# Feed-forward layers with the features on partitions, and transposes done by DMA, in a four-layer forward and backward pass

## The chip, the cores and the metric

The kernel runs on one core of one Trainium2 chip. The metric is device time in microseconds (us): the median of three runs of the whole program. A separate execution was taken by the hardware profiler; it has a time of its own, and its trace is what the lines below come from.

Engine names as the profile prints them: PE is the matmul engine (PEld is its weight load, which overlaps PE), DVE the vector engine, ACT the scalar engine, POOL the GpSimd engine, SP the queue that issues every DMA of this kernel.

## What is computed

Two kinds of layer alternate, A, B, A, B, on an activation of 2048 tokens by 512, with a residual and a layer norm in front of each; the program returns the output and the gradients with respect to the input and all five weights.

```python
def _A_ref(x, wqkv, wo):        # linear attention, 32 heads of 16
    qkv = x @ wqkv              # phi(t) = where(t > 0, t + 1, exp(t)) + 1e-6
    kv, z = sum_s phi(k) v, sum_s phi(k)
    return ((phi(q) @ kv) / (phi(q) . z + 1e-6)) @ wo
def _B_ref(x, w_gate, w_up, w_down):   # feed-forward, F = 1376
    return (sigmoid(x @ w_gate) * (x @ w_up)) @ w_down
x = x + A(ln(x)); x = x + B(ln(x)); x = x + A(ln(x)); x = x + B(ln(x))
out, vjp = jax.vjp(f, A_x, A_wqkv, A_wo, B_w_gate, B_w_up, B_w_down); grads = vjp(grad_out)
```

The change concerns the B layers (layers 1 and 3 of 0 to 3).

## The kernel before, in words

Tokens are cut into 16 tiles of 128 (`NST`), the model width into 4 chunks of 128 (`NDC`), F = 1376 into 10 chunks of 128 and one of 96 (`NFC`), or into slices of 512, 512 and 352 columns (`FSL`). The order of the instructions of PE, ACT, DVE and POOL is the order in which the program emits them (`tc.manual_schedule`, lines 134 and 1042 on); each engine works through its list in that order. Only SP's order is set by a scheduler. DMAs take turns on eight semaphores, and each waits for the one eight places ahead of it.

**Forward, layers A then B.** `kq_fwd` makes q and k of all tiles and sums over tokens; `ab_fwd` (from line 844) then walks over 16 token tiles and, tile by tile, does the rest of layer A and all of layer B, in a pipeline: while tile st is in B, tiles st+1 to st+3 are in A. For one tile of B, `gu` (line 857) makes gate and up with tokens on partitions: the normalised activations hT are stationary, 512 or 352 columns of w_gate and w_up move; ACT makes sigmoid(g) (`ssd`) and sigmoid(-g) (`oms`), DVE multiplies u by the sigmoid (`hh`, line 869), POOL makes the second factor of the derivative (line 870). `transposes` (line 872) turns `hh` on PE in 11 blocks, ACT copies them out (`hhT`), and `finish` (line 885) multiplies by w_down one tile later. Woven in are the fronts of layer A's output: `front1` (line 776) and `front2` (lines 786 to 788: three DVE instructions that make the normalised q, `pqn`), `front3` (PE transposes `pqn`, ACT copies it), `attn_y` (4 matmuls, DVE adds the residual, then layer norm statistics on DVE and POOL). In the middle of the walk, one tile's order is gu slice 2, `front2`, the transposes of slice 1, `finish` of the tile before (11 matmuls), `front3`. `Fill` places PE transposes of the weights (`wT_groups_a`, `wT_groups_b`) in between; the transposed weights are stored in DRAM and loaded again later.

**Backward, layer B.** `b_bwd_p1` (from line 1038) walks over token tiles: the output gradient's transpose `gT` (4 PE transposes, line 1000), `dhh_mm` (gT stationary, w_down transposed moving, line 1008), two DVE products per slice (`dd`, line 1016), 22 PE transposes of `dd` (line 1083) copied out by ACT (line 1085), 22 matmuls of 512 columns (line 1117) one tile later, and the layer norm's backward. `hh` and `dd` go to DRAM in groups of 256 features (`hdd`, the last 96 in `hdl`).

**Weight gradients.** `p2_gen` takes jobs of 256 (or 96) features. A job loads a set (`p_set`, line 1242: 16 token tiles by 256 features, 1 MB) and multiplies it with all tokens of h or of the gradient: 32 matmuls of 512 columns for w_down (line 1330), 64 of 256 columns for w_up or w_gate (line 1342). There are three set buffers; in the walk over jobs the next sets are issued about two jobs ahead. Jobs of layer 3 fill PE in the backward of layer A (`A2.first`) and then run alone; those of layer 1 do the same at the end of the program.

Of the kernel before, what the change touches and what calls it, by code (L numbers as in the profile page):

```python
# [17 lines left out]
S = 2048  # L18
# [9 lines left out]
FSL = [(0, 512), (512, 512), (1024, F - 1024)]  # L28
# [7 lines left out]
def fchunks_of_slice(fs):  # L36
    c0, w = FSL[fs]
    return list(range(c0 // P, (c0 + w + P - 1) // P))


def fc_rows(fc):
    return FLAST if fc == NFC - 1 else P
# [18 lines left out]
def kernel(  # L61
# [42 lines left out]
    for l in range(4):  # L104
        d = {}
        d["h"] = dram.tile([S, D], BF16, name=f"sv_h{l}")
        d["gbf"] = dram.tile([S, D], BF16, name=f"sv_gbf{l}")
        if l % 2 == 0:
            for nm in ("hT", "pqn", "phq", "pk"):
                d[nm] = dram.tile([S, D], BF16, name=f"sv_{nm}{l}")  # L110
            d["dqk"] = dram.tile([2 * D // GW, P, NST, GW], BF16, name=f"sv_dqk{l}")
            d["X"] = dram.tile([D, D], BF16, name=f"sv_X{l}")
            for nm, w in SMALL:
                d[nm] = dram.tile([D, w], BF16, name=f"sv_{nm}{l}")
            d["MT"] = dram.tile([D, D], BF16, name=f"sv_MT{l}")
        else:
            d["ssd"] = dram.tile([S, 2, F], BF16, name=f"sv_ssd{l}")
            d["hdd"] = dram.tile([3, NG, P, NST, GW], BF16, name=f"sv_hdd{l}")
            d["hdl"] = dram.tile([3, P, NST, F - NG * GW], BF16, name=f"sv_hdl{l}")
        k.sv[l] = d  # L120
    k.wT = dict(
        wqkvT=dram.tile([3 * D, D], BF16, name="wqkvT_d"),
        woT=dram.tile([D, D], BF16, name="woT_d"),
        wgT=dram.tile([NFC * P, D], BF16, name="wgT_d"),
        wuT=dram.tile([NFC * P, D], BF16, name="wuT_d"),
        wdT=dram.tile([D, F], BF16, name="wdT_d"),
    )
# [5 lines left out]
    )  # L133
    k.rstd = [keep.tile([P, NST], F32, name=f"rstd_all{l}") for l in range(4)]
# [5 lines left out]
    with tc.tile_pool(name="wfwd", bufs=1, reuse_waits="tile") as wfwd, ExitStack() as lctx, tc.manual_schedule(engines=EM):  # L140
# [25 lines left out]
        def load_wd():  # L166
            nc.sync.dma_start(out=k.wd[:, 0:NFC - 1, :],
                              in_=B_w_down[0:(NFC - 1) * P, :].rearrange("(c p) j -> p c j", p=P))
            for r0, r1 in ((0, 64), (64, FLAST)):
                nc.sync.dma_start(out=k.wd[r0:r1, NFC - 1, :],  # L170
                                  in_=B_w_down[(NFC - 1) * P + r0:(NFC - 1) * P + r1, :])
# [9 lines left out]
            hT=lctx.enter_context(tc.tile_pool(name="ln_hT", bufs=4, reuse_waits="tile")),  # L181
# [3 lines left out]
        with tc.tile_pool(name="aq0", bufs=1, reuse_waits="tile") as aq:  # L185
            A = kq_fwd(k, aq, 0, lns[0], lns[1], x_bf)
            with tc.tile_pool(name="wt_stage", bufs=2, reuse_waits="tile") as wt_stage:
                fill = Fill(wT_groups_a(k, wt_stage))
                A.tail(fill)
                ab_fwd(k, A, lns[1], fill, nxt=lns[2])  # L190
        xctx.close()
        with tc.tile_pool(name="aq2", bufs=1, reuse_waits="tile") as aq:
            A = kq_fwd(k, aq, 2, lns[2], lns[3])
            hctx.close()
            wb = bctx.enter_context(tc.tile_pool(name="wbwd", bufs=1, side="right", reuse_waits="tile"))
# [4 lines left out]

            def out_cb(st):
                if st == NB:
                    k.pre["g"] = pre.tile([P, 2, D], BF16, name="pre_g")
                    nc.sync.dma_start(out=k.pre["g"][:], in_=dram_batch(g_in, 0, 2))
                    k.pre["ssd"] = pre.tile([P, 2, F], BF16, name="pre_ssd")
                    nc.sync.dma_start(out=k.pre["ssd"][:], in_=k.sv[3]["ssd"][rows(0), :, :])
                if st % 2 == 0:
                    ocur["t"] = k.ostg.tile([P, 2, D], BF16, name="out0_t", bufs=2)
# [7 lines left out]
            def last_cb(i):  # L216
                if i == 0:
                    k.pre["gT"] = pre.tile([P, NDC, P], BF16, name="pre_gT")
                    g_transposes(k, k.pre["g"][:, 0, :], k.pre["gT"])
                else:  # L220
                    k.pre["dd"] = pre.tile([P, 2, F], BF16, name="pre_dd")
                    for fs in range(2):
                        dd_ops(k, k.pre["dd"], k.pre["ssd"], fs, dhh_mm(k, k.pre["gT"], fs))
            fill = Fill(wT_groups_b(k, wb))
            A.tail(fill)
            ab_fwd(k, A, lns[3], fill, out_cb=out_cb, last_cb=last_cb)
# [5 lines left out]
    if True:  # L232
        def load_b_weights():
            k.wdT = wb.tile([P, NDC, F], BF16, name="wdT", tag="w_c")
            nc.sync.dma_start(out=k.wdT[:], in_=k.wT["wdT"].rearrange("(c p) f -> p c f", p=P))
            k.wuT = wb.tile([P, NFC, D], BF16, name="wuT", tag="w_a")
            k.wgT = wb.tile([P, NFC, D], BF16, name="wgT", tag="w_b")
            for t_sb, t_d in ((k.wuT, k.wT["wuT"]), (k.wgT, k.wT["wgT"])):
                nc.sync.dma_start(out=t_sb[:], in_=t_d.rearrange("(c p) j -> p c j", p=P))

# [5 lines left out]
        def load_a_weights(l):  # L246
            nc.sync.dma_start(out=k.X_ld, in_=k.sv[l]["X"].rearrange("(c p) j -> p c j", p=P))
            k.wqkvT = wb.tile([P, 3 * NDC, D], BF16, name="wqkvT", tag="w_a")
            nc.sync.dma_start(out=k.wqkvT[:], in_=k.wT["wqkvT"].rearrange("(c p) j -> p c j", p=P))
            woT_GT = wb.tile([P, 2, NDC, D], BF16, name="woT_GT", tag="w_b")  # L250
            k.woT, k.GT = woT_GT[:, 0, :, :], woT_GT[:, 1, :, :]
            nc.sync.dma_start(out=k.woT, in_=k.wT["woT"].rearrange("(c p) j -> p c j", p=P))
        k.load_b_weights, k.load_a_weights, k.load_MT = load_b_weights, load_a_weights, load_MT
# [6 lines left out]
        def mk_out1_cb(o1stg):  # L260
            o1cur = {}

            def out1_cb(st):
                if st % 2 == 0:
                    o1cur["t"] = o1stg.tile([P, 2, D], BF16, name="out1_t")
                nc.gpsimd.tensor_scalar(o1cur["t"][:, st % 2, :], k.xs[st][:], 1.0, 0.0, ALU.mult, ALU.add)
                if st % 2 == 1:
                    nc.sync.dma_start(out=dram_batch(out1, st // 2, 2), in_=o1cur["t"][:])
            return out1_cb
# [3 lines left out]
        A2, A0 = ABwd(k, R, 2), ABwd(k, R, 0, mk_out1_cb)  # L273
# [82 lines left out]
def wT_groups_a(k, stage):  # L356
    nc = k.nc
    groups = []
    for w_sb, wT_d, C in ((k.wqkv, k.wT["wqkvT"], 3 * D), (k.wo, k.wT["woT"], D)):
        for cc0 in range(0, C // P, 4):  # L360
            holder = {}
            for j in range(4):
                def g(bank, w_sb=w_sb, wT_d=wT_d, cc0=cc0, j=j, holder=holder):
                    if j == 0:
                        holder["t"] = stage.tile([P, 4, D], BF16, name="wt_st")
                    cc = cc0 + j
                    ps = ps_tile(k, bank, [P, 8, P], BF16, "wT_ps")
                    for rc in range(NDC):
                        nc.tensor.transpose(ps[:, rc, :], w_sb[:, rc, cc * P:(cc + 1) * P], k.ident[:])

                    def ev(eng):
                        evac_copy(k, holder["t"][:, j, :], ps[:, 0:NDC, :].rearrange("p a b -> p (a b)"), eng)
                        if j == 3:
                            nc.sync.dma_start(
                                out=wT_d[cc0 * P:(cc0 + 4) * P, :].rearrange("(n p) d -> p n d", p=P),
                                in_=holder["t"][:])
                    return ev
                groups.append(g)
    return groups


def wT_groups_b(k, wb):
    nc = k.nc
    groups = []
    k.wdT = wb.tile([P, NDC, F], BF16, name="wdT", tag="w_c")
    k.wuT = wb.tile([P, NFC, D], BF16, name="wuT", tag="w_a")
    k.wgT = wb.tile([P, NFC, D], BF16, name="wgT", tag="w_b")
    for cc in range(NDC):
        for fs in range(3):
            def g(bank, cc=cc, fs=fs):  # L390
                fcs = fchunks_of_slice(fs)
                ps = ps_tile(k, bank, [P, 8, P], BF16, "wT_ps")
                for i, fc in enumerate(fcs):
                    r = fc_rows(fc)
                    nc.tensor.transpose(ps[:, i, 0:r], k.wd[0:r, fc, cc * P:(cc + 1) * P], k.ident[0:r, 0:r])
                c0, w = FSL[fs]

                def ev(eng):
                    evac_copy(k, k.wdT[:, cc, c0:c0 + w], ps[:].rearrange("p a b -> p (a b)")[:, 0:w], eng)
                    if cc == NDC - 1 and fs == 2:  # L400
                        nc.sync.dma_start(out=k.wT["wdT"].rearrange("(c p) f -> p c f", p=P), in_=k.wdT[:])
                return ev
            groups.append(g)
    for w_sb, wT_sb, wT_d in ((k.wu, k.wuT, k.wT["wuT"]), (k.wg, k.wgT, k.wT["wgT"])):
        for cc in range(NFC):
            def g(bank, w_sb=w_sb, wT_sb=wT_sb, wT_d=wT_d, cc=cc):
                r = fc_rows(cc)
                if cc == 0:
                    nc.gpsimd.memset(wT_sb[FLAST:P, NFC - 1, :], 0.0)
# [31 lines left out]
class FwdLN:  # L441
# [34 lines left out]
    def pop(self, st):  # L476
        return self.hTs.pop(st)
# [1233 lines left out]
```

## Time and profile before

| | us |
|---|---|
| median of 3 runs | 1213.65 (1212.94 to 1217.52) |
| profiled execution, its own time | 1216.08 |
| its span, first to last instruction | 1214.3 |
| PE / PEld busy in the span | 1185.4 / 716.8 |
| DVE / ACT / POOL busy | 726.9 / 599.9 / 259.1 |
| DMA engines busy, share | 66% |
| forward of layer 1 (first gate matmul to last w_down matmul) | 76.1 to 223.7 |
| forward of layer 3 | 281.1 to 432.5 |
| backward of layer 3 (dhh to dh matmuls) | 428.3 to 569.5 |
| jobs of layer 3 alone | about 715 to 793 |
| backward of layer 1 | 793.1 to 930.6 |
| jobs of layer 1 and layer 0 alone | about 1072 to 1210 |

How to read it: a matmul's end is modelled, so PE's busy time says that PE had something in flight; what a matmul costs in a stream is the distance from one start to the next. In a timeline line, the first column is the start, the second the length of the merged piece, `x4` the number of instructions, and brackets at the end give idle time of the engine before the piece and who ended it.

### The profile page before, as it was taken

What the parts mean: (1) busy time and instruction counts of PE and PEld (TensorE: products, weight loads), DVE (VectorE), ACT (ScalarE), POOL (GpSimd) and SP (SyncE); (2) the same over time, 40 slices, a digit from 0 to 9 for tenths busy, and PEclk for the clock granted to TensorE, in tenths of its full rate; (3) what the DMA queues carried; (4) which work ended last, traced back from release to release, by engine and by line L of the source; (5) the groups of instructions that cost most, each with busy time, mean ns of one, the idle gap of its engine ahead of it and who ended that gap; (6) DMA issues with size and microseconds to landing.
All of it is one profiled execution on the core that took longest, in us unless ns stands there. A gap on an engine that the chain in (4) does not pass through costs nothing. (4 is left out here: it accounts for less than half of the span.)

```text
span 1214.3 us, 22436 instructions
## 1 busy us (share of the span) xinstructions
PE 1185.4 (98%) x8646; PEld 716.8 (59%) x8646; DVE 726.9 (60%) x1410; ACT 599.9 (49%) x1105; POOL 259.1 (21%) x467
## 2 busy tenths in 40 slices
PE   7989999998999999999999999999999999999998
PEld 4445555454555555555665566765556755577777
DVE  6778887777777556565786730056666966742221
ACT  5677776647767644445537631145445527620001
POOL 4236675204665410000110010000100101100000
PEclk9999999999999999999999999999999999999999
DMA  7934545435546696967866469687667766569974
GB/s 231 311 118 144 197 157 181 172 122 176 185 150 231 232 279 184 312 187 236 229 188 203 147 222 322 206 281 218 213 194 246 206 219 180 170 172 351 293 234 135
DMA packets 266203, 256.08 MB, mean 211 GB/s; under 512 B 43248, under 2 KB 250992, under 8 KB 261232
## 3 DMA queue, kind: packets, MB, share of 16 engines
q1 hardware_dynamic: 266096, 254.65, 66.0%
q8 instruction: 67, 1.10, 0.4%
q14 instruction: 40, 0.33, 0.1%
HBM read 135.69 MB, written 118.92 MB: 210 GB/s over the span
## 5 line engine op out<-in xcount | busy, mean ns | idle before, releaser
L1342 PE MATMUL p_ps<-p_set,p_a 128*128 128x256 bf16 (+1 forms) x1792 | 186.8, 263 | 0.0
L1016 DVE TENSOR_TENSOR dd<-dhh_ps,ssd 128x512 bf16<-128x512 f32 x144 | 82.5, 629 | 149.0 <-PE dhh_ps L1008 142.1
L1342 PEld LDWEIGHTS <-p_a 128*128 128x128 bf16 x1792 | 160.3, 98 | 18.7
L1085 ACT COPY ddT<-T_ps 128x1024 bf16<-128x1024 bf16 (+1 forms) x96 | 82.9, 868 | 126.5 <-PE T_ps L1083 126.5
L870 POOL TENSOR_TENSOR ssd_t<-hh_t,oms 128x512 bf16<-128x512 bf16 (+1 forms) x96 | 101.6, 1064 | 53.6 <-ACT out_t L212 40.9
L1117 PEld LDWEIGHTS <-ddT 128*128 128x128 bf16 (+1 forms) x704 | 66.4, 98 | 68.6
L864 PEld LDWEIGHTS <-hT 128*128 128x128 bf16 x768 | 71.2, 98 | 57.8 <-DVE hT L341 1.5
L982 POOL TENSOR_SCALAR ab<-c 128x2 f32<-128x2 f32 x64 | 12.5, 196 | 433.2 <-DVE junk L979 416.4
L864 PE MATMUL g_ps<-wg,hT 128*128 128x512 bf16 (+1 forms) x384 | 90.0, 357 | 1.1 <-DVE hT L341 1.1
L1321 DVE TENSOR_TENSOR dw_stg<-p_ps,dw_stg 128x512 bf16<-128x512 f32 (+2 forms) x43 | 28.4, 659 | 103.3 <-PE p_ps L1342 80.8
L864 PE MATMUL u_ps<-wu,hT 128*128 128x512 bf16 (+1 forms) x384 | 90.0, 357 | 0.0
L869 DVE TENSOR_TENSOR hh_t<-u_ps,ssd_t 128x512 bf16<-128x512 f32 (+1 forms) x96 | 61.0, 636 | 46.9 <-PE u_ps L864 26.7
L1117 PE MATMUL dh_ps<-wgT,ddT 128*128 128x512 bf16 (+1 forms) x352 | 86.2, 379 | 0.0
L1008 PE MATMUL dhh_ps<-wdT,gT 128*128 128x512 bf16 x372 | 82.5, 357 | 0.5 <-DVE dd L1016 0.5
L890 PE MATMUL y_ps<-wd,hhT 128*128 128x512 bf16 (+1 forms) x352 | 81.3, 379 | 0.6 <-DVE x L892 0.6
L1117 PE MATMUL dh_ps<-wuT,ddT 128*128 128x512 bf16 (+1 forms) x352 | 81.3, 379 | 0.0
L1330 PE MATMUL p_ps<-p_a,p_set 128*128 128x512 bf16 (+1 forms) x352 | 80.4, 379 | 0.0
L866 ACT ACTIVATE ssd_t<-g_ps 128x512 bf16<-128x512 f32 (+1 forms) x96 | 53.2, 554 | 31.7 <-PE g_ps L864 31.4
L974 ACT ACTIVATE t_sb<-dh_ps,rstd_all 128x512 f32<-128x512 f32 x64 | 44.0, 688 | 36.6 <-issue 18.4
L979 DVE SCALAR_TENSOR_TENSOR junk<-t_sb,h_ld 128x512 bf16<-128x512 f32 x60 | 41.2, 687 | 34.8 <-ACT t_sb L974 34.8
L1323 ACT CAST dw_stg<-p_ps 128x512 bf16<-128x512 f32 (+2 forms) x43 | 24.2, 563 | 72.1 <-PE p_ps L1342 51.8
L1330 PEld LDWEIGHTS <-p_set 128*128 128x128 bf16 (+1 forms) x352 | 34.4, 100 | 35.5
(236 smaller groups left out, 2184.9 us busy)
## 6 DMA issues: line engine op xcount, KB each, us to landing
p_set<-sv_hdd SPq DMA_DIRECT2D x30, 1024.0 KB, 6.4
sv_ssd<-ssd_t SPq DMA_DIRECT2D x32, 688.0 KB, 3.5
ssd<-sv_ssd SPq DMA_DIRECT2D x24, 688.0 KB, 5.0
sv_hdd<-dd SPq DMA_DIRECT2D x48, 320.0 KB, 3.3
sv_hdd<-hh_t SPq DMA_DIRECT2D x32, 320.0 KB, 2.6
p_set<-sv_dqk SPq DMA_DIRECT2D x8, 1024.0 KB, 5.4
h_ld<-sv_h SPq DMA_DIRECT2D x30, 256.0 KB, 4.5
p_a<-sv_h SPq DMA_DIRECT2D x12, 512.0 KB, 6.5
```

The costliest lines, as they stand in the source:

```text
L864: nc.tensor.matmul(ps[:, 0:w], lhsT=hT[:, kc, :], rhs=w_sb[:, kc, c0:c0 + w], start=(kc == 0), stop=(kc == NDC - 1))
L866: nc.scalar.activation(ssd_t[:, 0, c0:c0 + w], g_ps[:, 0:w], ACT.Sigmoid)
L869: nc.vector.tensor_tensor(hh_t[:, c0:c0 + w], u_ps[:, 0:w], ssd_t[:, 0, c0:c0 + w], ALU.mult)
L870: nc.gpsimd.tensor_tensor(ssd_t[:, 1, c0:c0 + w], hh_t[:, c0:c0 + w], oms[:, 0:w], ALU.mult)
L890: nc.tensor.matmul(y_ps[:], lhsT=T["hhT"][0:r, fc, :], rhs=k.wd[0:r, fc, :], start=(fc == 0), stop=(fc == NFC - 1))
L974: k.nc.scalar.activation(self.t[:], dh_ps, ACT.Identity, scale=rstd_col, accum_out=self.c12[:, 0:1])
L1008: k.nc.tensor.matmul(ps[:, 0:w], lhsT=gT[:, jc, :], rhs=k.wdT[:, jc, c0:c0 + w], start=(jc == 0), stop=(jc == NDC - 1))
L1016: k.nc.vector.tensor_tensor(dd[:, a, c0:c0 + w], ps[:, 0:w], ssd[:, a, c0:c0 + w], ALU.mult)
L1085: nc.scalar.copy(ddT[:, :, fcs[0]:fcs[0] + nfull, :], tps[:, :, 0:nfull, :])
L1117: nc.tensor.matmul(T["dh"][:], lhsT=T["ddT"][0:r, a, fc, :], rhs=(k.wuT, k.wgT)[a][0:r, fc, :], start=(i == 0), stop=(i == 2 * NFC - 1))
L1330: nc.tensor.matmul(ps[0:r, :], lhsT=set_t[:, st, j * P:j * P + r], rhs=g_all[:, st, :], start=(st == 0), stop=(st == NST - 1))
L1342: nc.tensor.matmul(ps[:, icl * w:(icl + 1) * w], lhsT=h_all[:, st, ic * P:(ic + 1) * P], rhs=set_t[:, st, 0:w], start=(st == 0), stop=(st ...
```

## The change

- **Forward of B** goes over 8 pairs of tiles. The weights are now stationary (blocks of 128 features) and 256 tokens move, so gate, up and `hh` come out with features on partitions and no transpose of `hh` is needed. The last feature chunk is taken as the last 128 columns, with the 32 that overlap zeroed in w_down, w_up^T and w_gate^T. A pair is 6 steps (`CPAIRS`: five of two chunks, one of one chunk). The order of the woven-in work is new; `stage_T`'s copy moves from DVE to ACT.
- **Weights** are transposed by DMA from the inputs, instead of by PE with a store and loads; `Fill` and both `wT_groups` are gone.
- **Backward of B**: `gT` comes by a transposing DMA; `dhh` has w_down^T stationary and 256 tokens moving, so `dd` has features on partitions and needs no transposes on PE nor copies by ACT. The 22 matmuls per tile stay, cut into pieces between the `dhh` steps.
- **DRAM layout**: `hd` is kept as features by tokens; a job's set is loaded by a transposing DMA. `ssd` is stored and loaded in 12 pieces a pair (two planes of 512 or 256).
- The gradient between layers 2 and 1 is stored by the callback of `ABwd.second` on POOL, instead of in `b_bwd_p1`.

Core of the diff (lines of "..." are left out):

```diff
+def wide_mm(k, ps, lhs, rhs, j):
+    c0, n = CPAIRS[j]
+    for i in range(n):
+        f0 = fcol(c0 + i)
+        for kc in range(NDC):
+            k.nc.tensor.matmul(ps[:, i, :], lhsT=lhs[:, kc, f0:f0 + P], rhs=rhs[:, kc, :],
+                               start=(kc == 0), stop=(kc == NDC - 1))
...
+        def gu(U, j):
...
+            for nm, w_sb in (("g", k.wg), ("u", k.wu)):
+                ps = ps_tile(k, nm, [P, 2, PW], F32, f"{nm}_ps")
+                wide_mm(k, ps, w_sb, U["hT"], j)
...
+            s_t = wide.tile([P, 2, 2 * PW], BF16, name="ssd_t", bufs=4)
+            nc.scalar.activation(s_t[:, 0, 0:w], g_ps, ACT.Sigmoid)
...
+            nc.vector.tensor_tensor(hh, u_ps, s_t[:, 0, 0:w], ALU.mult)
+            nc.gpsimd.tensor_tensor(s_t[:, 1, 0:w], hh, oms[:, 0:w], ALU.mult)
+            nc.sync.dma_start(out=sv["ssd"][U["p"], :, :, c0:c0 + n, :], in_=ssd_view(s_t, n))
...
+            else:
+                gu(U, 0)
+                A.attn_y(a + 2)
+                A.prod(a + 4)
+                gu(U, 1)
+                A.attn_y(b + 2)
+                A.front1(a + 4)
+                A.prod(b + 4)
+                finish(prev, 0)
+                gu(U, 2)
+                A.front2(a + 4)
+                ln.apply(a + 2)
+                A.front3(a + 4)
+                if not last:
+                    finish(prev, 1)
+                gu(U, 3)
+                A.front1(b + 4)
+                ln.apply(b + 2)
+                after(prev, 0)
+                ln.stage_T(a + 2)
+                gu(U, 4)
+                A.front2(b + 4)
+                A.front3(b + 4)
+                if not last:
+                    after(prev, 1)
+                ln.stage_T(b + 2)
+                gu(U, 5)
...
+            ins = hd_store(k, l, 0, p, U["hhT"])
...
-    def tail(fill):
+    def tail():
         A.ln.apply(0)
-        A.attn_mm(1)
-        fill("gugu", "scalar")
-        A.front2(2)
         A.ln.stage_T(0)
-        A.attn_add(1)
-        A.extra = fill.mm("t")
+        A.ln.apply(1)
+        A.ln.stage_T(1)
+        A.front2(2)
+        A.front1(3)
+        A.front2(3)
+        A.prod(4)
...
+def dd_make(k, dd, gT, ssd, j):
+    c0, n = CPAIRS[j]
+    ps = ps_tile(k, "gu"[j % 2], [P, 2, PW], F32, "dhh_ps")
+    wide_mm(k, ps, k.wdT, gT, j)
     for a in range(2):
-        k.nc.vector.tensor_tensor(dd[:, a, c0:c0 + w], ps[:, 0:w], ssd[:, a, c0:c0 + w], ALU.mult)
+        k.nc.vector.tensor_tensor(dd[:, a, c0:c0 + n, :], ps[:, 0:n, :], ssd_view(ssd, n)[:, a, :, :], ALU.mult)
...
+            gTs[p] = gtp.tile([P, NDC, PW], BF16, name="gT")
+            nc.sync.dma_start_transpose(out=gTs[p][:], in_=sv["gbf"][pair_cols(p), :])
...
+        PIECES = ((0, 0, 7), (0, 7, 15), (0, 15, 22), (1, 0, 7), (1, 7, 15), (1, 15, 22))
...
+            for j in range(NJ):
+                i = p * NJ + j
+                ssd_next(i + 4)
+                if not (first and i < 2):
+                    dd_make(k, U["dd"], gTs[p], ssds[i], j)
...
+                    dh_mm(prev, *PIECES[j])
...
+            for a in range(2):
+                hd_store(k, l, 1 + a, p, U["dd"][:, a, :, :])
...
+    def load_wdT():
+        k.wdT = k.wb.tile([P, NDC, F], BF16, name="wdT", tag="w_c")
+        nc.sync.dma_start_transpose(out=k.wdT[:], in_=B_w_down)
...
-def p2_set(k, R, src):
+def p2_set(k, R, src, w, transposed):
     t = R.sets.tile([P, NST, R.set_w], BF16, name="p2_set")
-    R.eng().dma_start(out=t[:, :, 0:src.shape[-1]], in_=src)
+    if transposed:
+        k.nc.sync.dma_start_transpose(out=t[:, :, 0:w], in_=src)
+    else:
+        R.eng().dma_start(out=t[:, :, 0:w], in_=src)
     return t
```

## The prediction

> **What bounds the kernel now.** The first view is the page's engine table, against a span of 1214.3 us and an own time of the profiled execution of 1216.08.
>
> ```profile
> PE 1185.4 (98%) x8646; PEld 716.8 (59%) x8646; DVE 726.9 (60%) x1410; ACT 599.9 (49%) x1105; POOL 259.1 (21%) x467
> ```
>
> PE has work in flight nearly always, so every PE instruction removed counts, unless PE then waits for something. The second view, the chain of work that ended last, gives what a matmul costs in a stream.
>
> ```profile
> 1095.44 6.91 PE p_ps L1330 x32
> 1102.35 13.97 PE p_ps L1342 x128
> ```
>
> 6.91 / 32 = 0.216 us for 512 columns, 13.97 / 128 = 0.109 for 256. The third view is PE's timeline in the middle of the forward walk, where starts one after the other give a transpose: 4 in 0.22, 0.055 each.
>
> ```profile
> 154.52 0.76 PE L864 MATMUL u_ps<-wu,hT 128*128 128x352 bf16 x4
> 155.12 0.39 PE L878 MATMUL t_tp<-ident,hh_t 128*128 128x128 bf16 x4
> 155.34 2.54 PE L890 MATMUL y_ps<-wd,hhT 128*128 128x512 bf16 x11
> 157.75 0.40 PE L334 MATMUL ln_tp<-ident,pqnstage 128*128 128x128 bf16 x4
> ```
>
> Between the u matmuls (done by 155.12) and the transposes of `pqn` at 157.75 stand 11 matmuls of `finish`. DVE's timeline shows what they cover:
>
> ```profile
> 155.39 0.53 DVE L869 TENSOR_TENSOR hh_t<-u_ps,ssd_t 128x352 bf16<-128x352 f32 x1
> 155.83 0.55 DVE L786 TENSOR_SCALAR den<-den 128x32 f32<-128x32 f32 x1
> 156.42 0.35 DVE L787 RECIPROCAL rden_all<-den 128x32 f32<-128x32 f32 x1
> 156.80 0.90 DVE L788 TENSOR_TENSOR pqnstage<-pq_all,rden_all 128x512 bf16<-128x512 bf16 x1
> ```
>
> `pqn` is ready at 157.70, 0.05 before PE takes it up. In the first tile there is no tile before, hence no `finish`, and the same chain is bare:
>
> ```profile
> 82.53 0.39 PE L369 MATMUL wT_ps<-ident,wqkv 128*128 128x128 bf16 x4
> 84.72 0.40 PE L334 MATMUL ln_tp<-ident,pqnstage 128*128 128x128 bf16 x4 [1.80 <-DVE pqnstage L788]
> ```
>
> PE idles 1.80 us. This wait returns below.
>
> **The change, part by part.**
>
> *Removed from PE.* Transposes of `hh` (352), `dd` (704), the weights (196) and `gT` (128): 1380 x 0.055 = 76 us. If nothing stood in its place the time would be about 1138. The columns of the real matmuls stay: 512 columns by 0.216 and 256 by 0.109 cost the same.
>
> *Forward.* PE work of a pair: 88 x 0.109 = 9.6 (gate, up), 22 x 0.216 = 4.75 (`finish`), 8 x 0.216 = 1.73 (attention output), 16 x 0.055 = 0.9; 16.95 in all. Before, two tiles take 18.43 (`hh` of one tile starts at 150.92, of the next at 160.14: 9.22 each). But the new order is gu(2), `front2`, `front3`, and only then `finish(prev, 1)`; and gu(4), `front2`, `front3`, then `stage_T`. So PE finds the transposes of `pqn` directly behind gate and up, while DVE must first do `hh` (0.69, it starts some 0.27 after PE as above), then `den`, reciprocal, `pqn`. That chain lasts 0.17 + 0.35 + 0.69 with POOL quiet (first tile) and 0.55 + 0.35 + 0.90 beside POOL (above), with the hand-overs 2.1 to 2.75 from the last matmul; I take 2.45, twice a pair. The cover that hid it is gone, and what is queued behind the waiting transposes on PE is all of the pair: `finish`, gu(3). The transposes of b + 2 also wait for ACT's copy of the one `ln_tp` bank (0.91), and the next gu(0) for their own copy (0.25): 1.16. A pair with both fronts (p = 1 to 5) is then 16.95 + 4.9 + 1.16 = 23.0. Pair 0 is 12.65 + 4.4 = 17.05, pair 6 (no front) 17.4, pair 7 14.35, the last `finish` 5.2: 169 a layer. Before it is 76.1 to 223.7 (147.6) and 281.1 to 432.5 less 1.7 of dhh (149.7): **+21.4 and +19.3**. Ahead of the walk gu(0) now waits for the hT copies of two tiles instead of one, 1.2 a layer: **+2.4**. Without the two stalls the walk would be some 25 us a layer shorter. Fill's transposes and the copies of hT off DVE are in the counts already; ACT has room (49%).
>
> *Backward of B.* A layer needs 352 x 0.109 = 38.4 (dhh) and 352 x 0.216 = 76.0 (dh and up's half), 114.4 us, with 2.2 to 3.3 for the first pair, where DVE leads. Here pieces of matmuls of the pair before stand between the dhh steps, so each product of DVE has cover; DVE needs 12.3 of a pair's 14.3 us. Before: 432.5 to 569.5 (137.0, of which 1.7 now lies ahead) and 793.1 to 930.6 (137.5). **-22.1 and -19.8.** So on PE's side -42 and +43, **+1.2** in sum.
>
> *DMA.* Here two windows speak, columns as span, PE, PEld, DVE, ACT, POOL, clock, DMA share, GB/s.
>
> ```profile
> 428.00:570.00 142.00, 140.36 (x983) 78.09 (x981) 86.70 (x159) 66.03 (x116) 4.64 (x18) 1.00 0.77 237
> 1100.00:1120.00 20.00, 20.00 (x157) 15.26 (x156) 4.34 (x7) 0.00 (x0) 0.00 (x0) 1.00 1.05 355
> ```
>
> The backward moves 0.77 x 142 = 109 us of transfers, which are to fit into some 118: a share of about 0.9. The trace has slices of 0.9 with PE at work and none that says what two such backwards cost; between nothing and 6 a layer (its gain would be cut by a third) I take 3 each, **+6**.
>
> `p_set` by a transposing DMA is the unknown. Today:
>
> ```profile
> p_set<-sv_hdd SPq DMA_DIRECT2D x30, 1024.0 KB, 6.4
> ```
>
> as 128 x 8 KB, at 390.7 ns a packet, 3.1 us of 16 engines. No transposing DMA is in the trace. Nearest row: packets of 256 B, one row of a 128-wide block, take 18.1 ns; 4,096 of them 4.6 us. Low end: as now, 3.1. High end: pieces of 32 B at the price of the smallest packet seen (4 B, 8.7 ns): 32,768 x 8.7 / 16 = 17.8. I take 4.6, nearest in kind. A set may take 7.0 us (32 x 0.216, or 64 x 0.109) before PE waits. Some 26 sets are loaded where jobs run alone (715 to 793, 1072 to 1178). In the second stretch the DMA share is 0.9, 0.9 and 0.7 in the slices of the page; 13 sets x 1.5 us more on about 90 us of transfers make 110 in 106: **+5** with the lesser overrun of the first. SP issues 799 DMAs instead of 721 in one queue, on eight semaphores that take turns, so the issue of a short load can stand behind a long transpose: **+2**, between 0 and 6. Weights (five matrices at the start) are loaded beside the forward, whose DMA share is 0.3 to 0.6: nothing; without that cover some 8 us once.
>
> [...]
>
> *Sum.* 1216.1 + 1.2 + 6 + 5 + 2 = 1230.3 against the profiled execution, which stands 2.4 above the median of the runs: **1228**.
>
> **The rivals.**
>
> 1. *The chain is covered after all.* If DVE could have `pqn` ready when PE comes to it, the forward would be about 25 us a layer shorter: 1228 - 50 = 1178, with pair boundaries met as well 1170. For it: `front1` and `prod` are done long before. Against: `front2` stands behind `hh` in DVE's list, and the bare case at 84.72 is in the trace. 0.10. A half (one of the two waits covered, or the chain nearer 1.2 us): 1200. 0.12.
> 2. *Transposing sets bind* (the other side of the bound). Their place is the stretches where jobs run alone, their price a set's time above 7.0 us, their point of decision 7.0. At 9.2, twice the value taken, 26 x 2.2 = 57: 1285. For it: no such DMA is in the trace and the ends lie far apart. Against: the nearest row is 4.6. 0.20. At 17.8, 26 x 10.8 = 281: about 1510. 0.06.
> 3. *DVE and POOL get in each other's way.* `den` takes 0.17 with POOL quiet and 0.55 beside POOL's product of 1.15 us, `pqn` 0.69 and 0.90; if all 20 waits see the busy price, 20 x 0.3 over the mean = +6: 1234, inside the forecast's own range. [...]
>
> **How the numbers follow.** Forecast 0.52 (its own range 1212 to 1246), rival 1 0.22, rival 2 0.26. A measurement tells about half a percent, 6 us, from no change: 1207.6 to 1219.7. Of the forecast's 0.52 some 0.14 lie within that, 0.04 below, 0.34 above. Faster 0.04 + 0.22 = 0.26, same 0.14, slower 0.34 + 0.26 = 0.60. The range 1182 to 1300 leaves out the fully covered chain (0.10), the far price (0.06) and a little of the nearer one.
>
> **What would show it.** In PE's timeline of pairs 1 to 5, two idle stretches of 1.5 to 2.5 us ahead of L334's transposes, released by DVE `pqnstage`; a pair's period of 23; the backward of a layer at 115 to 121, with PE busy; the transposing `p_set` at 4 to 5 us of DMA time, and the alone stretches near their old lengths. The forecast is wrong if a pair takes 17 to 18, or if PE in the alone stretches waits for `p_set`.

## The result, and the profile after

The changed kernel takes 1303.49 us (median of 4 runs, 1301.46 to 1305.71) against 1214.18 in the same comparison: 1.073 times as long, 95% interval 1.070 to 1.076. Forecast were 1228 and a range up to 1300. The profiled execution took 1301.46, its span is 1299.7.

The changed kernel's page, engine table, clock and DMA rows (40 slices of 32.5 us, tenths):

```profile
PE 1160.1 (89%) x8113; PEld 752.1 (58%) x8226; DVE 707.1 (54%) x1342; ACT 453.7 (35%) x834; POOL 258.8 (20%) x470
PEclk8988889999978999989999999999999999999999
DMA  7833324443445657999898759999995997489994
```

PE is busy for 25 us less and idle for 140 us instead of 29, and the granted clock (PEclk, a share of full speed) is down at 0.7 to 0.8 in slices 2 to 5 and 11 and 12, counted from 0, inside the two forward walks. Cutting the span at the same places of the program as before shows where the time came from (last column: the best variant, e10_spread, below):

| stretch, us | before | after | difference | forecast | e10_spread |
|---|---|---|---|---|---|
| up to the first gate matmul | 76.1 | 77.8 | +1.7 | +1.2 | 75.6 |
| forward of layer 1 | 147.6 | 191.1 | +43.5 | +21.4 | 146.6 |
| layer 2, q and k | 57.4 | 59.1 | +1.7 | +1.2 | 59.2 |
| forward of layer 3 | 151.4 | 185.5 | +34.1 | +17.6 | 146.9 |
| backward of layer 3 | 137.0 | 125.8 | -11.2 | -20.4 | 114.5 |
| backward of layer 2, jobs of layer 3 | 223.6 | 243.5 | +19.9 | +7 with the last row | 244.4 |
| backward of layer 1 | 137.5 | 116.4 | -21.1 | -19.8 | 116.5 |
| the rest (backward of layer 0, jobs) | 283.7 | 300.5 | +16.8 | in the +7 | 301.0 |

(The forecast's +6 for DMA in the two backwards is not spread over rows; its 1.7 of dhh is counted in the rows where the cuts lie.) Three things are off: the forward, the jobs, and the backward of layer 3. The windows of the changed kernel for these stretches say which engine misses what (span, PE, PEld, DVE, ACT, POOL, granted clock, DMA share, GB/s):

```profile
77.80:268.90 191.10, 155.14 (x1042) 107.01 (x1057) 103.38 (x188) 84.38 (x154) 93.10 (x145) 0.88 0.37 121
328.00:513.50 185.50, 147.88 (x1051) 103.50 (x1066) 94.89 (x161) 79.91 (x152) 79.86 (x104) 0.94 0.56 163
513.50:639.30 125.80, 117.69 (x688) 68.96 (x699) 84.34 (x154) 13.26 (x33) 4.04 (x17) 0.96 1.01 274
779.00:882.80 103.80, 93.37 (x686) 66.65 (x688) 6.53 (x13) 18.14 (x33) 2.96 (x7) 0.97 1.06 237
882.80:999.20 116.40, 115.60 (x710) 70.16 (x721) 86.25 (x157) 13.85 (x34) 3.42 (x16) 1.00 0.91 262
1142.00:1299.70 157.70, 142.33 (x1225) 111.71 (x1228) 29.70 (x48) 7.04 (x12) 0.62 (x1) 0.98 0.96 224
```

The same columns before, for the forward of layer 1 and for the stretch in which the jobs of layer 3 run alone:

```profile
76.10:223.70 147.60, 144.93 (x961) 78.66 (x962) 116.33 (x219) 105.37 (x207) 94.44 (x150) 1.00 0.49 170
703.40:793.10 89.70, 89.12 (x695) 65.97 (x693) 7.00 (x13) 18.82 (x34) 3.18 (x6) 1.00 0.79 263
```

In the forwards of the changed kernel PE is idle for some 37 us each with DMA about half empty, and what it does it does at a mean clock of 0.88 and 0.94. In its job stretches (fourth and last line) the DMA share is about 1 and PE idles 10 and 15 us. The backward of layer 1 is the one stretch where PE is full, and there the forecast holds to about a microsecond. PE's timeline over most of one forward pair (start, length, matmuls, in brackets the idle time ahead and its releaser):

```profile
143.85 1.04 PE L799 MATMUL u_ps<-hT,wu 128*128 128x256 bf16 x8
148.15 0.61 PE L347 MATMUL ln_tp<-ident,pqnstage 128*128 128x128 bf16 x4 [3.27 <-DVE pqnstage L741]
149.43 0.59 PE L347 MATMUL ln_tp<-ident,hstage 128*128 128x128 bf16 x4 [0.67 <-ACT pqnT L356]
149.81 1.06 PE L799 MATMUL g_ps<-hT,wg 128*128 128x256 bf16 x4
150.66 1.06 PE L799 MATMUL u_ps<-hT,wu 128*128 128x256 bf16 x4
151.51 1.92 PE L799 MATMUL g_ps<-hT,wg 128*128 128x256 bf16 x8
153.22 1.49 PE L799 MATMUL u_ps<-hT,wu 128*128 128x256 bf16 x8
...
161.27 1.04 PE L799 MATMUL u_ps<-hT,wu 128*128 128x256 bf16 x8
164.46 0.61 PE L347 MATMUL ln_tp<-ident,pqnstage 128*128 128x128 bf16 x4 [2.15 <-DVE pqnstage L741]
165.28 3.56 PE L837 MATMUL yd_ps<-wd,hhT 128*128 128x512 bf16 x10 [0.22 <-issue]
```

The two bare waits are there, 3.27 and 2.15 us. New is what follows them: four gate matmuls take 0.85 (149.81 to 150.66), 0.213 each instead of 0.109, and the tile of `finish` at 165.28 takes 3.4 us instead of 2.4. The granted clock is 0.50 from 147.31 to 154.13 and from 164.37 to 167.78, and 1.00 between.

The slow matmuls do not follow every wait. Three pairs of layer 3, each from one `pqn` transpose to the same one of the next pair:

```profile
358.73:386.84 28.11, 21.39 (x133) 14.18 (x135) 13.09 (x22) 10.65 (x20) 10.72 (x14) 0.81 0.54 146
413.79:439.25 25.46, 18.75 (x132) 12.84 (x134) 13.09 (x22) 10.51 (x20) 10.72 (x14) 0.94 0.60 162
439.25:463.18 23.93, 17.38 (x132) 12.32 (x135) 13.09 (x22) 10.51 (x20) 10.73 (x14) 1.00 0.54 167
```

The bare waits in them are the same, 3.08 and 2.69 us; only the clock differs, and with it the pair, 28.1 to 23.9. Of the 20 bare waits of the two forwards 13 have a half-rate stretch at their end or within some 2 us of it, 7 have none. The waits as a whole:

```profile
PEld L347 <- DVE pqnstage L741: 66.6, 26, 3.5
```

Before, the same transposes waited 10.4 us in all, 16 times:

```profile
PEld L334 <- DVE pqnstage L788: 10.4, 16, 2.0
```

### The profile page after: what moved, and what is told of

Read it like the earlier page. It is cut to its first block, busy times and chain, and to the rows that moved or that the text cites. A ratio compares the mean times of both kernels' runs of the same rounds, so it can differ in the third digit from the quotient of the medians.

```text
span 1299.7 us, 21424 instructions
## 1 busy us (share of the span) xinstructions
PE 1160.1 (89%) x8113; PEld 752.1 (58%) x8226; DVE 707.1 (54%) x1342; ACT 453.7 (35%) x834; POOL 258.8 (20%) x470
## 5 line engine op out<-in xcount | busy, mean ns | idle before, releaser
L960 DVE TENSOR_TENSOR dd<-dhh_ps,ssd_ld 128x512 bf16<-128x512 f32 x144 | 85.4, 640 | 121.5 <-PE dhh_ps L799 107.4
L828 POOL TENSOR_TENSOR ssd_t<-hhT,oms 128x512 bf16<-128x512 bf16 x96 | 103.0, 1073 | 152.8 <-DVE hhT L827 89.2
L799 PE MATMUL g_ps<-hT,wg 128*128 128x256 bf16 x704 | 103.0, 292 | 4.3 <-ACT hT L356 4.3
L823 ACT ACTIVATE ssd_t<-g_ps 128x512 bf16<-128x512 f32 x96 | 54.2, 565 | 146.9 <-PE g_ps L799 145.5
L799 PE MATMUL u_ps<-hT,wu 128*128 128x256 bf16 x704 | 100.5, 288 | 0.0
L799 PE MATMUL dhh_ps<-gT,wdT 128*128 128x256 bf16 x660 | 86.6, 274 | 7.4 <-DVE pre_dd L960 4.8
L799 PEld LDWEIGHTS <-wdT 128*128 128x128 bf16 x704 | 69.0, 98 | 34.9 <-DVE pre_dd L960 5.3
L799 PEld LDWEIGHTS <-wg 128*128 128x128 bf16 x704 | 72.8, 105 | 25.8 <-issue 5.8
L837 PE MATMUL yd_ps<-wd,hhT 128*128 128x512 bf16 x336 | 85.3, 407 | 1.6 <-issue 0.9
L799 PEld LDWEIGHTS <-wu 128*128 128x128 bf16 x704 | 73.1, 104 | 11.9
L1027 PE MATMUL dh_ps<-wgT,dd 128*128 128x512 bf16 x258 | 64.4, 386 | 0.4
```

The costliest lines, as they stand in the source:

```text
L799: k.nc.tensor.matmul(ps[:, i, :], lhsT=lhs[:, kc, f0:f0 + P], rhs=rhs[:, kc, :], start=(kc == 0), stop=(kc == NDC - 1))
L823: nc.scalar.activation(s_t[:, 0, 0:w], g_ps, ACT.Sigmoid)
L828: nc.gpsimd.tensor_tensor(s_t[:, 1, 0:w], hh, oms[:, 0:w], ALU.mult)
L837: nc.tensor.matmul(y_ps[:], lhsT=U["hhT"][:, fc, half * P:(half + 1) * P], rhs=k.wd[:, fc, :], start=(fc == 0), stop=(fc == NFC - 1))
L960: k.nc.vector.tensor_tensor(dd[:, a, c0:c0 + n, :], ps[:, 0:n, :], ssd_view(ssd, n)[:, a, :, :], ALU.mult)
L1027: nc.tensor.matmul(U["dh"][half][:], lhsT=U["dd"][:, a, fc, half * P:(half + 1) * P], rhs=(k.wuT, k.wgT)[a][:, fc, :], start=(i == 0), sto ...
```

## The experiments

Theories. **A**: the forward loses by the two bare waits of a pair and, in about equal parts, by the half-rate matmuls behind them. **B**, its rival: another engine or SP holds the pair. **C**: the job stretches lose because a transposing load holds SP. **D**, its rival: they lose because the DMA engines need longer for its small pieces.

### The order in the forward (e1_order)

```diff
                 A.front1(a + 4)
+                A.front2(a + 4)
                 A.prod(b + 4)
                 finish(prev, 0)
                 gu(U, 2)
-                A.front2(a + 4)
...
                 A.front1(b + 4)
+                A.front2(b + 4)
...
                 gu(U, 4)
-                A.front2(b + 4)
-                A.front3(b + 4)
...
                 gu(U, 5)
+                A.front3(b + 4)
```

> The changed kernel with another order in the forward pairs 1 to 7 and nothing else: the three DVE instructions that make pqn stand right behind the reduction of den, ahead of the next gate and up step, and the transposes of the second tile's pqn move behind gu(5), with the hT transposes of b + 2 ahead of gu(5). Theory A: the forward of B loses 79 us against before because PE waits for pqn twice a pair (66.6 us of waits) and because the granted clock falls to half for some microseconds behind each wait (mean 0.88 and 0.94). Then both go: a pair falls from 27.5 to about 17 to 18, a forward from 191 and 185 to 135 to 145, the time from 1303 to about 1205 to 1220. Rival B: the pair is held by something else as well (DVE, POOL, or SP, which is held 2.3 us by each store of ssd): a pair stays above 22, the time above 1255.

Measured: 1224.64 us, 1.007 times before (1.005 to 1.010). The forwards take 148 and 148 us, a pair 18.4. The waits and the half rate of A go together and B falls: 79 us of the 89 are gone, by order alone. A's sizes were too good: expected were 1205 to 1220 and a pair of 17 to 18. What is left in a pair is short:

```profile
128.22 1.04 PE L799 MATMUL u_ps<-hT,wu 128*128 128x256 bf16 x8
129.46 0.38 PE L347 MATMUL ln_tp<-ident,hstage 128*128 128x128 bf16 x4 [0.20 <-ACT hT L356]
129.68 0.60 PE L799 MATMUL g_ps<-hT,wg 128*128 128x256 bf16 x4
130.11 0.60 PE L799 MATMUL u_ps<-hT,wu 128*128 128x256 bf16 x4
131.62 0.38 PE L347 MATMUL ln_tp<-ident,pqnstage 128*128 128x128 bf16 x4 [0.91 <-ACT hT L356]
```

Behind the wait of 0.20 us four matmuls take 0.43 (129.68 to 130.11): full rate. Behind the one of 0.91 it is full as well (eight in 0.87, from 131.84).

### Waits or clock: useless matmuls in the waits (e5_busy)

```diff
+                busy(a + 4, 10)
                 A.front3(a + 4)
...
+                busy(b + 4, 14)
                 A.front3(b + 4)
```

`busy` multiplies the identity with w_down, 512 columns a time, into a bank that nobody reads.

> The changed kernel with useless matmuls added: ahead of each pqn transpose in the forward pairs 1 to 5, 10 or 14 matmuls of 512 columns (2.2 and 3.0 us) into a PSUM bank that nobody reads. PE still gets pqn no sooner, so the wait as such stays, filled. Theory A (half the loss is the clock, which falls to half because PE stands idle): the clock stays at 1.00, a pair falls from 27.5 to about 23, and the whole from 1303 to about 1265 to 1275, although PE does 240 matmuls more. Rival: the slow matmuls behind the wait are slow for another reason (their operands, SBUF or PSUM traffic): the added matmuls then cost 0 to 50 us, 1303 to 1350.

Measured: 1279.08 us (ratio to before 1.052, 1.049 to 1.054), 24 us less than the changed kernel, though PE does 240 matmuls more. The forwards:

```profile
76.40:250.50 174.10, 164.07 (x1157) 110.01 (x1176) 103.58 (x189) 83.53 (x154) 92.88 (x144) 0.99 0.41 133
310.20:487.30 177.10, 165.68 (x1164) 111.67 (x1183) 94.67 (x161) 79.78 (x152) 79.90 (x104) 0.99 0.61 171
```

The clock is 0.99 instead of 0.88 and 0.94, and PE's timeline shows the matmuls behind the (now filled) wait at full rate, four in 0.44:

```profile
160.15 3.19 PE L857 MATMUL warm_ps<-wd,ident 128*128 128x512 bf16 x13
163.58 0.40 PE L347 MATMUL ln_tp<-ident,pqnstage 128*128 128x128 bf16 x4 [0.24 <-DVE pqnstage L741]
164.65 0.38 PE L347 MATMUL ln_tp<-ident,hstage 128*128 128x128 bf16 x4 [0.67 <-ACT pqnT L356]
164.87 0.60 PE L799 MATMUL g_ps<-hT,wg 128*128 128x256 bf16 x4
165.31 0.60 PE L799 MATMUL u_ps<-hT,wu 128*128 128x256 bf16 x4
```

The transposes of `pqn` come no sooner than in the changed kernel (the pair's two spans from the start of the last u matmuls to them are 4.3 and 3.2 us in both), so it is not the waits that became shorter, and the rival, slow matmuls for another reason, falls. Of the +78 us of the two forwards about 25 (17.0 and 8.4) are matmuls at half rate, and the rest is the waits: a third, not the equal parts of theory A. A pair takes 23.7 us in layer 1 and 23.9 in layer 3, the latter as in the changed kernel's own pairs at full clock; the forecast, which knew only the waits, had 23.0, and 169 for a forward against 174 and 177. The expected 1265 to 1275 was missed by 4: it took half rate behind the waits of every pair (27.5 us), and in layer 3 the pairs fall from 28.1 to 23.9 by themselves.

### Transposing sets: hold of SP or small pieces (e2_plain256, e3_plain4k)

```diff
-        k.nc.sync.dma_start_transpose(out=t[:, :, 0:w], in_=src)
+        k.nc.sync.dma_start(out=t[:, :, 0:w].rearrange("q n (a t) -> q n a t", t=P),
+                            in_=src.rearrange("(a q) (n t) -> q n a t", q=P, t=P))
```

e3_plain4k instead reads each feature's 2048 tokens in one piece of 4 KB. Both leave out the transposition, so three weight gradients come from operands that lie the wrong way; the matmuls stay, and so do the bytes, but for the smaller set of each gradient, which is loaded with 128 features instead of 96.

> The changed kernel, the sets of the feed-forward weight gradients loaded by plain DMAs in the same 256-byte pieces (features stay on partitions, so these three gradients are computed from the wrong operand; same bytes, same matmuls). Theory C: the weight-gradient stretches lose 37 us (103.8 against 89.7, 157.7 against 141.8, and 7 in the backward of A) because each transposing set holds SP for 5.2 us instead of 0.4, so that other loads come late: the time falls to about 1265 to 1275. Rival D: the DMA engines need longer for 4,096 pieces of 256 bytes (22.2 ns each, 5.7 us a set, instead of 3.1): nothing changes, 1295 to 1305.

> As the run before, but the plain loads of the 1 MB sets go in pieces of 4 KB (the three gradients again from the wrong operand; same bytes, same matmuls). Theory C (SP held): about the same as with plain loads of 256-byte pieces, 1265 to 1275. Rival D (cost of the small pieces in the DMA engines): here alone the time falls, to about 1265, and the plain 256-byte loads stay near 1300.

Measured: 1289.8 (1288.26 to 1296.5) and 1269.65 us (1269.14 to 1272.53), against 1303.49: 14 us gained without the transposition, 20 more without the small pieces. Both theories have a part. SP's queue of the changed kernel, in the last stretch (start, how long SP was held, transfer):

```profile
1207.45 5.42 SPq L1150 DMA_TRANSPOSE p_set<-sv_hd  x1
1212.97 0.53 SPq L1207 DMA_DIRECT2D out_dram<-dw_stg  x1
1213.55 0.46 SPq L1209 DMA_DIRECT2D dw_stg<-dwp_wg  x1
1214.06 0.57 SPq L1573 DMA_DIRECT2D XT_ld<-sv_XT  x1
1214.67 0.51 SPq L1573 DMA_DIRECT2D kvbd_ld<-sv_kvbd  x1
1215.27 5.58 SPq L1150 DMA_TRANSPOSE p_set<-sv_hd  x1
```

and the same queue before:

```profile
1110.51 0.51 SPq L1299 DMA_DIRECT2D dw_stg<-dwp_wd  x1
1111.12 0.45 SPq L1242 DMA_DIRECT2D p_set<-sv_hdd  x1
```

A transposing set holds SP for a median of 5.4 us, a plain one before for 0.33 (in e2_plain256 for 0.6), and from 1207 on SP goes from one issue to the next with gaps of no more than 0.1 us. In the trace's packets the set is 4,096 pieces of 256 bytes. The mean of all packets of that size in the run is 22.2 ns in the changed kernel and 22.2 in e2_plain256 too, which makes an estimate of 22.2 x 4,096 / 16 = 5.7 us of all engines for a set, against 3.1 before. The last stretch of e2_plain256 and of e3_plain4k, 150 us each:

```profile
1125.00:1275.00 150.00, 139.93 (x1141) 104.40 (x1145) 35.57 (x60) 10.68 (x21) 3.23 (x8) 0.97 0.98 230
```

```profile
1110.00:1260.00 150.00, 149.26 (x1278) 115.36 (x1284) 39.27 (x66) 13.35 (x26) 3.85 (x9) 1.00 0.78 242
```

With SP free but small pieces the DMA share stays 0.98 and PE idles 10 us; with 4 KB pieces the share is 0.78 and PE is full. There D decides: from the end of the backward of layer 1 on, the three take 300.5 (changed), 297.7 and 283.9. In the stretch of the layer 3 jobs both plain forms gain alike (243.5 to 229.7 and 230.2), so there the size of the pieces is not what costs, and SP's hold is the difference that is left; it is argued, no run takes it away alone. The stretches of e2_plain256 are from an execution of 1296.5 us, the longest of its five and 6.7 above their median: its backward of layer 1 (125.4, 9 us more than in the changed kernel) need not be typical.

### Part of the load taken away elsewhere (e4_wT, e7_both)

In e4_wT the transposed weights are stored once and loaded plainly the second time; in e7_both also the forward order of e6_order2 (below) is used.

```diff
+        if not again("wdT", k.wdT):
             nc.sync.dma_start_transpose(out=k.wdT[:], in_=B_w_down)
+            keep_T("wdT", k.wdT)
```

> The changed kernel, the transposed weights (w_gate, w_up, w_down, the q, k and v matrix) stored after the first transposing load and fetched by plain DMAs the second time, as the kernel before did from its own copies. In the stretch where jobs of layer 3 run alone (779 to 883) their transposing loads hold SP for 21 us and lie in the DMA queue among nine sets. If that stretch is bound by what SP and the DMA engines have to do (rivals C and D agree here): it falls from 104 to about 93 to 97, the time from 1303 to about 1292 to 1297. If the sets alone are the matter, nothing changes (1300 to 1306).

> Forward order of e6_order2 and the stored weights of e4_wT together. The two lie in different stretches, so their gains should add: about 1198 to 1208, which would be below the kernel before.

Measured: 1296.96 (1293.14 to 1302.74) and 1218.55 (1216.22 to 1220.62). Alone the edit is 6.5 below the changed kernel, in the expected 1292 to 1297 but with ranges that overlap, and the stretch that was to gain 7 to 11 us (backward of layer 2, jobs of layer 3) gives 2 (243.5 to 241.6), so the theory behind it is not shown. With the mended forward the edit gives nothing (e6_order2: 1217.4), where 1198 to 1208 were expected. The gains did not add: in e7_both the jobs' stretch is 4 us shorter and the forward of layer 3, where the extra stores are issued, 5 us longer.

### A second step in the order (e6_order2)

Against e1_order, in pairs 1 to 7 (pair 0 is changed to match):

```diff
                 gu(U, 0)
+                A.front3(b + 2)
                 A.attn_y(a + 2)
...
                 gu(U, 5)
-                A.front3(b + 4)
```

> The mended forward order (e1_order), with the transposes of the second tile's pqn moved once more, behind gu(0) of the next pair. In e1_order a pair takes 18.4 us against 16.95 of PE work, and PE's waits in the pair are 0.2 and 0.9 us ahead of the transposes into the one ln_tp bank, behind ACT's copies. Theory: with gu(0) between them the bank is free and a pair falls to 17.0 to 17.5; 10 to 12 pairs give 10 to 17 us, 1224.6 to about 1208 to 1215. Rival: what is left of the pair is set by another engine (DVE or ACT), and the time stays within 4 us of 1224.6.

Measured: 1217.4 us (1214.63 to 1221.13): 7 less than e1_order, not 10 to 17. The wait of 0.91 us was not removed but moved; now gu(0) itself waits for its hT:

```profile
165.74 0.60 PE L799 MATMUL u_ps<-hT,wu 128*128 128x256 bf16 x4
167.25 1.03 PE L799 MATMUL g_ps<-hT,wg 128*128 128x256 bf16 x8 [0.91 <-ACT hT L356]
```

### The burst in the backward of layer 3 (e10_spread)

PE's timeline of the changed kernel there:

```profile
576.66 1.04 PE L799 MATMUL dhh_ps<-gT,wdT 128*128 128x256 bf16 x4 [4.83 <-DVE pre_dd L960]
577.49 3.19 PE L1027 MATMUL dh_ps<-wgT,dd 128*128 128x512 bf16 x7
583.28 1.03 PE L799 MATMUL dhh_ps<-gT,wdT 128*128 128x256 bf16 x8 [2.59 <-DMA gT<-in_grad_out_dram]
```

Two waits; seven matmuls of 512 columns behind the first take 3 us instead of 1.5. SP issued ahead of them, in one go:

```profile
556.77 2.39 SPq L1143 DMA_DIRECT2D p_a<-sv_h  x4
559.21 6.38 SPq L1143 DMA_DIRECT2D p_a<-in_grad_out_dram  x4
565.69 4.60 SPq L784 DMA_DIRECT2D ssd_ld<-sv_ssd  x3
```

```diff
-            if mid is not None and i == 4 * NJ:
+            if mid is not None and i >= 2 * NJ and i % 3 == 0:
                 with tc.issue_after(ins.ins):
-                    mid()
+                    next(mid, None)
```

> As e6_order2, and in the backward of layer 3 the eight 512 KB loads of the weight-gradient operands (p_a) are issued one by one, every third step from pair 2 on, instead of all in one burst of 9 us of SP at pair 4. Theory: that backward takes 126 us instead of the 115 that PE needs (layer 1: 116) because the short loads of ssd and gT, only four steps ahead, stand behind the burst: PE waits 4.8 and 2.6 us there and then runs at a lower clock (0.69 in that slice). Then the stretch falls to 115 to 119 and the time from 1217.4 to about 1207 to 1211. Rival: the stretch is bound by its bytes (DMA share 1.01), and the loads come late wherever they stand: within 3 us of 1217.4.

Measured: 1205.79 us (1204.56 to 1206.49), 0.991 times before (0.989 to 0.993): the fastest of all that keep the computation. The stretch:

```profile
427.90:542.40 114.50, 113.82 (x688) 68.17 (x700) 83.96 (x154) 13.26 (x33) 4.04 (x17) 1.00 1.06 294
```

The same bytes in less time, at a DMA share of 1.06, and PE is full: not the bytes but the burst was the cost.

### Does another order of the jobs recover the rest? (e9_mix, e12_mix2, e15_mix3, e16_mix4, e13_actq)

If the DMA engines are full while transposed sets follow one another and idle in the plain jobs behind them, jobs of both kinds in turn should gain. All four mixes do that; each mends what spoiled the one before.

```diff
+            if i % 4 == 3:
+                for _ in range(8):
+                    next(w1, None)
```

(12 instead of 8 in e9_mix.)

> As e7_both, and at the end of the program the jobs of layer 1 (transposed sets) take turns with those of layer 0 (plain sets), three to one, instead of all layer 1 jobs first. Same bytes, same matmuls. Theory D (there the DMA engines are the bound: 14 sets x 5.7 us of 256-byte pieces, DMA share 0.96 to 1.00, and the jobs of layer 0 behind them leave them idle): 4 to 10 us below e7_both. Rival C (SP's hold ahead of short loads) or a latency that each set has: within 3 us of e7_both.

> As e10_spread, and the jobs of layer 1 take turns with those of layer 0 at the end, as in e9_mix, but only after two or more whole jobs of layer 1, so that the last transposes of layer 0 (fin_ps) again have jobs between them and the operand t_a of layer 0 is loaded before its first job; both were missing in e9_mix (PE busy 7 of the 20 us from 1060). Theory D (the last stretch is bound by DMA time, and the plain sets of layer 0 at its end leave the DMA engines idle): 4 to 10 us below e10_spread. Rival: within 3 us of e10_spread, or above it.

> As e12_mix2, with the small gradients (sg_ps) moved to the last two jobs of layer 0, since in e12_mix2 PE stood 5.5 and 3.4 us for their operand kvbd_ld at 1115 to 1119 and then ran at a lower clock (0.57 in that slice), while behind that point PE was busy 19 to 20 of 20 us at DMA shares of 0.76 to 0.94. Theory D (the DMA engines are full while transposed sets follow one another): without that wait the mix gains 4 to 8 us on e10_spread, 1198 to 1202. Rival (the mix gives nothing, each set has its own latency): 1204 to 1209.

> As e15_mix3, with the loads of the small gradients' operands issued later, one at a time between the sets: in e15_mix3 eight of them and a plain set stood ahead of one transposing set in SP's order (1105 to 1119), and PE waited 14.3 us for it, while behind that point PE was busy 20 of 20 us. Theory D (DMA time is the bound while transposed sets follow one another, so plain sets in between recover part): 4 to 10 us below e10_spread (1205.8), 1196 to 1202. Rival (the order of the jobs gives nothing): 1204 or more.

Measured: 1226.51 against e7_both's 1218.55, and 1211.63, 1215.24 and 1212.72 against e10_spread's 1205.79. None gained; in each PE stands for a load that comes late: 5.7 us for `t_a` in e9_mix, 8.8 for `kvbd_ld` in e12_mix2, and in e15_mix3:

```profile
1127.47 9.02 PE L1282 MATMUL p_ps<-p_set,p_a 128*128 128x256 bf16 x64 [14.29 <-DMA p_set<-sv_hd]
```

In e16_mix4 that wait is 7.84 us. Behind the long wait of e15_mix3 PE was busy for 39.95 of 40 us at DMA shares of 0.85 and 0.90, so part of what D says is seen, but no order that I found turns it into time.

e13_actq asks the same of C: the partial sums are loaded through ACT's queue, past SP.

```diff
-                R.eng().dma_start(out=t, in_=d)
+                nc.scalar.dma_start(out=t, in_=d)
```

> As e10_spread, and the partial sums that a job of layer 1 or 0 adds to (dw_stg, 256 KB each) are loaded through ACT's DMA queue instead of SP's, so that they no longer stand behind a transposing set on SP. Theory C (SP's hold of 5.2 to 5.6 us a set is what makes these loads late; DVE waits 68 us in all for them, and PE 10 us for DVE): the last stretch falls by 6 to 12 us. Rival D (the DMA engines are full, with 4,096 small pieces a set): within 3 us of e10_spread.

Measured: 1207.37 us (1203.19 to 1210.76), no difference from e10_spread; 6 to 12 us less were C's expectation. The loads themselves are no longer late: from the end of the backward of layer 1 on, DVE waits 67 us for them in e10_spread and not at all in e13_actq, where it waits for PE instead (52 us there, 106 here). So SP's hold did make these loads late, but their lateness does not cost the time: PE waits only some 7 us for DVE there and 4 here, and the last stretch goes from 301.0 to 298.9.

### What the transposing sets cost in the end (e14_floor)

> As e10_spread, with the sets of the feed-forward weight gradients loaded by plain DMAs of 4 KB pieces (these three gradients from the wrong operand; same bytes, same matmuls). It shows what the transposing sets still cost when the forward and the burst are mended. Theory D: as in e3_plain4k some 34 us, 1168 to 1176. If the cost was part of the other stalls: less than 20, 1186 or more.

Measured: 1176.73 us (1174.48 to 1179.85), with the transposition left out as in e3_plain4k: 29 below e10_spread, a little under the 34 of e3_plain4k. The jobs' stretches fall to 230.9 and 284.3, close to before's 223.6 and 283.7; the rest stays.

## Why the prediction was wrong, point by point

The profiled execution took 71 us more than the 1230.3 that the prediction's sum has for it: 39 in the forwards, 30 in the job stretches and 6 in the backward of layer 3, less 4 in that of layer 1.

- **The bare waits in the forward: right.** Two per pair, released by DVE `pqnstage`, as forecast; filled with work (e5_busy) a pair takes 23.7 and 23.9 against 23.0, and mended (e1_order) 79 us are gone.
- **The step that failed first: "A pair with both fronts (p = 1 to 5) is then 16.95 + 4.9 + 1.16 = 23.0."** It prices all PE work at 0.109 and 0.216, also behind a wait. The trace of before, at a mean clock of 0.999, shows one bare wait of 1.80 us with full rate behind it, and I took that for the rule. Behind 13 of the 20 waits of 2.15 to 3.27 us matmuls run at half rate, which e5_busy shows to be about 25 of the 39 us. The waits themselves were longer too: 2.15 and 3.27 us in a pair of layer 1, 2.69 and 3.08 in one of layer 3, against 2.45 each, which makes 7 us over all 20. In the one of 3.27 DVE stood 1.27 us for ACT's sigmoid, a wait the chain left out, and `pqn` took 1.32. In the half-rate stretches the granted clock is 0.50 and a matmul of 256 columns takes 0.213 instead of 0.109; those that follow the waits last 3.4 or 6.8 us. What sets them off is not shown: behind a wait of 2.15 us one begins (164.46) or none (191.95), and behind one of 3.08 us too (one at 369.98, none at 424.90, 448.83 and 472.75), so the length of a wait alone does not decide.
- **The sets: the mechanism was rival 2, its point of decision was wrong.** I took 4.6 us a set, a point of decision of 7.0, and +5. The set takes some 5.7 us of DMA, below 7.0, and still costs: other loads and stores share the engines (share 0.96 to 1.06), and SP is held 5.4 us a set, where I had +2 for all of SP (in the last stretch the hold made loads late at no cost, e13_actq). Together +37 instead of +7; e2_plain256 and e3_plain4k divide their 34 into 14 for the transposition and 20 for the pieces, e14_floor leaves 29 in the mended kernel. At 5.7 us, an estimate from the 22.2 ns of a packet under load, 1 MB moves at 184 GB/s.
- **The backward: right for layer 1** (-21.1 against -19.8), with no DMA loss at a share of 0.91. For layer 3 the forecast of 3 us of DMA was 11: not a share, but a burst of eight loads ahead of short ones (e10_spread).
- **The rivals.** The chain covered after all (1170) fell with the first timeline. The trace agrees with DVE and POOL in each other's way (rival 3), at more than its price: 15 of the 20 `pqn` products have POOL's wide product (L828) beside them and take 1.21 to 1.32 us, the other five, in layer 1, take 0.69. The forecast had 0.90 at most. In the first tile before, which the chain took for quiet, a narrower product of POOL's (L870, 352 columns) ran from 84.01, and `pqn`, from 83.97, still took 0.69, so standing side by side alone does not decide. No run separates it from the rest of the wait.
- **What stays open.** Why mixing the jobs never gains although the windows show idle DMA time behind them: each mix met a late load, and no run separates that from the set's own latency. Also why the clock falls behind one wait and not behind the next of the same length.

## What to carry to other kernels

A transpose removed from the bound engine is a gain only if nothing stood on it: here `finish` and the transposes of `hh` covered a DVE chain, and the order that lost that cover cost as much (79 us, e1_order) as all the transposes were forecast to save (76). Price an idle stretch of PE of 2 to 3 us in two ways, with and without slower matmuls behind it (0.213 and 0.109 here), and if it can't be mended, try filling it (24 us less in e5_busy). A transposing load can be paid for in DMA time and in its queue's hold (here some 5.7 us, an estimate, and 5.4 us a set); whether a load that it makes late costs anything has to be tried, as here it cost nothing in one stretch. Spread large loads that have time (11 us in the backward of layer 3, e10_spread).

## What the runs showed of the hardware

- 240 useless matmuls made the program 24 us faster (e5_busy: 1279.08 against 1303.49).
- Bare waits of 3.08 us in the changed kernel's trace had matmuls at half rate behind them (369.98) and matmuls at full rate (448.83); the half-rate stretches in the forwards last 3.4 or 6.8 us each.
- The changed kernel's transposing loads of the sets held their queue for a median of 5.4 us (plain: 0.33 before, 0.6 in e2_plain256), and the run's 256-byte packets took 22.2 ns in the mean, the same with the sets loaded plainly in pieces of that size.
- The backward of layer 3 ran with PE full at a DMA share of 1.06 (e10_spread), and lost 11 us at 1.01 with a burst in it: the share alone did not tell.
